# Attention beside a dense branch on one core: key tiles through one query half, then the other, seven score units beside twelve products, and a division on 128x32 sums

## The chip, the core and the metric

One of the cores of a Trainium2 chip runs the whole kernel. Its engines are TensorE (PE; PEld are its weight loads, which run beside the products), VectorE (DVE), ScalarE (ACT), GpSimd (POOL), and SyncE (SP), which issues most of the DMAs. Each engine works off its own queue in order, and semaphores let one wait for another. Products go to PSUM, eight banks of 128 x 512 floats. The metric is the device time of one execution in microseconds. All times below are from one profile and three runs of the kernel before; "a unit", "a phase" and "a pair" are explained with the kernel.

## The reference

Two branches on the same input x (2048 rows, 512 columns) are mixed by a gate. Branch A is attention with 32 query heads of 16 columns and one shared key and value head; branch B is a dense layer, a squared ReLU, and a second dense layer.

```python
def _A_ref(x, wq, wk, wv, wo):          # H = 32, Dh = 16
    q = (x @ wq).reshape(B, S, H, Dh).transpose(0, 2, 1, 3)
    k = x @ wk
    v = x @ wv
    scores = jnp.einsum("bhqd,bkd->bhqk", q, k) * (Dh ** -0.5)
    p = _softmax(scores, axis=-1)
    o = jnp.einsum("bhqk,bkd->bhqd", p, v)
    return o.transpose(0, 2, 1, 3).reshape(B, S, H * Dh) @ wo
def _B_ref(x, w1, b1, w2, b2):          # F = 1792
    h = jnp.einsum("bsd,df->bsf", x, w1) + b1
    r = jnp.where(h > 0, h, 0)
    return jnp.einsum("bsf,fd->bsd", r * r, w2) + b2
x = A_x
g = _sigmoid((x * gate_w).sum(-1, keepdims=True))
return g * _A_ref(x, ...) + (1 - g) * _B_ref(x, ...)
```

## The kernel before

**Attention.** The 2048 queries lie in four chunks of 512, the 32 heads in eight groups of four: 32 iterations (`it`, `NC * NG`), and in each 16 key tiles of 128 keys (`kt`). A **unit** `u` is one key tile with one half of the 512 queries (256 columns) for all four heads, so an iteration has 32 units and the kernel 1024 (`place`, L738). In every iteration but the last, a key tile's two halves follow each other; in the last, all key tiles run through the first half and then through the second.

A unit's scores are two products of 49 rows (`score`, L753), one in each half of the rows of TensorE's array (r = 0 and r = 1), which run beside each other; each half holds two heads. They go to a PSUM tile `s` of two banks (two of them take turns), and ScalarE writes their exponentials to SBUF (`exps`, L781). Some units are "raw": each half goes to the single bank `x`, VectorE copies it to SBUF (`score_copy`, L770), and ScalarE then exponentiates in place. The exponentials lie in five tiles `e` of two units each. The contexts (`context`, L797) multiply them with the values and a column of ones (`v_ext`), for the four heads beside each other in four groups of the array's columns, and add up in one bank `acc`: heads in rows 32h and on, values and sums of the exponentials in alternating rows. Before, two units of one key tile share products of 512 columns.

**The other products.** The queries' projection (15 pieces), the dense branch and the output projection are split into a rounded part and the rest (`split`, L191; names ending in r and l), so that a tile needs three products for each pair of tiles. A piece of this work with one PSUM bank `mm` (a span, `Span`) has 12 products, some have 9, the last ones fewer. A product of 128 rows is done in two halves of 64 rows: the first half of one span runs beside the second half of the span before, so a step of TensorE is always a **pair** of row halves, either of products or of scores.

**The order.** `manual_schedule` keeps each engine's instructions as they are written. The program is a sequence of **phases** (`phase`, L1138): the scores of some units and the products of a span, interleaved by a table (`PLANS`; M is a product, S0 a unit's scores, 02 and 12 the two halves of raw unit 2), and behind them the contexts of as many units, which were scored up to four units ahead (`AHEAD`). `block` (L1191) chooses how many units and products a phase takes: six or four units here, and no phase crosses the end of an iteration. A planner keeps rough clocks (`at_pe`, `at_act`, `at_dve`) and puts VectorE's other work (`spend`, L622: rests of weights, chores, divisions) between the copies of raw scores. Work for DMAs has due times (`LANDS`, `DIVIDES`, `WRITES`).

**The division.** When an iteration ends, `finish` (L836) copies acc to SBUF on ScalarE; two DMAs take the values to `oc` and the sums of exponentials to `lc`, one row of 512 sums for every row of values (the sums of a head stand 16 times). After two iterations `divide` (L821) works on six slices of at most 86 columns: bound the sums, compare with what was bounded (its count, `ok`, tells at the end whether the shift of the exponents sufficed), reciprocal, product with the values. A POOL DMA writes `oc` to DRAM (`oTs`), from where the output projection reads.

Of the kernel before, what the change touches and what calls it, by code (L numbers as in the profile page):

```python
# [10 lines left out]
F32 = mybir.dt.float32  # L11
# [12 lines left out]
NG = 8  # L24
# [10 lines left out]
PARTS = [slice(a, min(a + 86, CH)) for a in range(0, CH, 86)]  # L35
LANDS, DIVIDES, WRITES, SURE = 6.0, 10.0, 14.0, 0.7
# [20 lines left out]
LAST_OK = (NC * KT - 1) * len(PARTS)  # L57
# [106 lines left out]
def mix_kernel(ctx: ExitStack, tc: tile.TileContext, xT, wkv, wq, wo, w12, b1, b2, cst, out):  # L164
# [7 lines left out]
    qs = dram.tile([NC * NG, 2, KS, 2, CH], F32, name="qs")  # L172
    oTs = dram.tile([NC * NG, 64, CH], F32, name="oTs")
# [7 lines left out]
    ok = keep.tile([128, NC * KT * len(PARTS)], F32, name="ok")  # L181
# [46 lines left out]
    with fast, tc.tile_pool(name="at", bufs=1) as at, \  # L228
# [381 lines left out]
        def later(f, *args):  # L610
            chores.append((1.2, lambda: f(*args)))
# [85 lines left out]
        def x_again(c):  # L697

            r, l = [xp.tile(sh, F32R, name=f"x{n}again{c}", tag=f"x{n}{c - 2}") for n in "rl"]
            def load(a):  # L700
                nc.sync.dma_start(stage()[:, :2], xT[c, 2 * a:2 * a + 2].rearrange("k p s -> p k s"))
                return LANDS

            def part(k):
                split(r[:, k], l[:, k], stage()[:, k % 2])
                if k == KT - 1:
                    x[c] = r, l

            for k in range(KT):
                if k % 2 == 0:  # L710
                    chores.append((0.0, lambda k=k: load(k // 2)))
                later(part, k)
# [84 lines left out]
        def context(acc, us):  # L797

            nonlocal at_pe
            at_pe += 0.12  # L800
            while us:
                u, (it, kt, q) = us[0], place(us[0])
                n = 2 if u % 2 == 0 and len(us) > 1 and it < NC * NG - 1 else 1
                at_pe = max([at_pe] + [made[i] + 0.06 for i in us[:n]]) + CONTEXT * n
                us = us[n:]
                cols, mine = slice(q * HC, (q + n) * HC), slice(u % 2 * HC, (u % 2 + n) * HC)
                for h in range(4):
                    nc.tensor.matmul(acc[h * 32:(h + 1) * 32, cols], v_ext[:, kt],  # L808
                                     es[u // 2][:, h % 2 * 2 + h // 2, mine], start=(kt == 0), stop=(kt == NK - 1),
                                     skip_group_check=True, tile_position=(0, h * 32))  # L810
            if narrow:
# [9 lines left out]
        def divide(o, l, cols, okc):  # L821

            n = []

            def bound():
                n.append(at.tile([128, 86], F32, name="n")[:, :cols.stop - cols.start])
                nc.vector.tensor_scalar(n[0], l[:, cols], L_MIN, L_MAX, op0=OP.max, op1=OP.min)

            def compare():
                nc.vector.scalar_tensor_tensor(l[:, cols], n[0], 1.0, l[:, cols], op0=OP.mult, op1=OP.is_equal,  # L830
                                               accum_out=okc)

            return ((0.23, bound), (0.35, compare), (0.72, lambda: nc.vector.reciprocal(n[0], n[0])),  # L833
                    (0.28, lambda: nc.vector.tensor_tensor(o[:, cols], o[:, cols], n[0], OP.mult)))

        def finish(it, acc):  # L836

            c, gr = divmod(it, NG)
            t, u = divmod(gr, 2)
            if it == NC * NG - 2:  # L840
                a = at.tile([128, CH], F32, name="al", tag="accs")
                nc.vector.tensor_copy(a, acc)
                side.append(turn(a, 0, range(4), LAST_OK))
                return
            a = at.tile([128, CH], F32, name="accs")
            nc.scalar.activation(a, acc, AF.Copy)
            act(0.62, at_pe)
            if u == 0:
                ol[c, t] = [at.tile([128, CH], F32, name=n, bufs=2) for n in ("oc", "lc")]
            o, l = ol[c, t]  # L850
            unpack(nc.sync, o[u * 64:u * 64 + 64], l[u * 64:u * 64 + 64], a)
            if u == 1:
                for q, cols in enumerate(PARTS):
                    i = len(PARTS) * (4 * c + t) + q
                    divisions.extend((d, at_act + (LANDS if (c, t) == (NC - 1, 2) else DIVIDES), f) for d, f in divide(o, l, cols, ok[:, i:i + 1]))

                def done():
                    nc.gpsimd.dma_start(oTs[it - 1:it + 1].rearrange("u d n -> (u d) n"), o)
                    complete.add((c, t))

                divisions.append((0.0, 0.0, done))
# [27 lines left out]
        def half(acc, q):  # L889
# [3 lines left out]
            nc.vector.tensor_copy(a[:, :HC], acc[:, q * HC:q * HC + HC])  # L893
# [21 lines left out]
            if q:  # L915
                nc.vector.tensor_scalar(bad, pf, 128.0 * ((NC * KT - 1) * CH + 32) - 0.5, None, op0=OP.is_lt)
# [14 lines left out]
        def o_ready(c):  # L931

            if c == 0 and not wos:
                wos.extend(xp.tile(sh, F32R, name=n, tag=t) for n, t in (("wor", "xr2"), ("wol", "xl2")))

                def load(a):
                    nc.sync.dma_start(stage()[:, :2], wo[a * 256:a * 256 + 256].rearrange("(t p) n -> p t n", p=128))
                    return WRITES

                for t in range(KT):  # L940
                    if t % 2 == 0:
                        chores.append((0.0, lambda t=t: load(t // 2)))
                    later(split, wos[0][:, t], wos[1][:, t], stage()[:, t % 2])
            if c > 0:
                ask(c - 1)

        def ask(c, n=KT):
# [15 lines left out]
            def part(t):  # L963
                orr, orl = tiles
                split(orr[:, t], orl[:, t], stage()[:, t % 2])
                if t == n - 1:
                    osp[c] = orr, orl

            for t in range(n):
                if t % 2 == 0:  # L970
                    chores.append((0.0, lambda t=t: load(t // 2)))
                later(part, t)

        def ask_one(c, t):
# [10 lines left out]
            def part():  # L985
                split(osp[c][0][:, t], osp[c][1][:, t], stage()[:, 0])
                osp[c, t] = True

            chores.extend(((0.0, load), (1.2, part)))
# [23 lines left out]
        def work():  # L1013
# [61 lines left out]
            units_left[0] = 0  # L1075
# [5 lines left out]
        side, units = [], work()  # L1081
# [108 lines left out]

        def block(u):  # L1191
# [8 lines left out]
            if span.done[0] == 0 and left > 9:  # L1200
                halved[0] += max(0.0, (total - 20 - u - 6 * units_left[0]) / (1.6 * max(units_left[0], 1)))
            if rest == 8 or rest == 4 or left > 9 and halved[0] >= 1.0 and rest not in (6, 10) and not late:
                halved[0] -= 1.0
                return 4, (left + 1) // 2
            return min(rest, 6), left

        late, halved, units_left = [], [0.5], [NC * (NF + 16) + 15 + 16]

        acc, us = None, ()
# [9 lines left out]
        u = 0  # L1219
        while u < total:  # L1220
            it, k = divmod(u, 2 * NK)
            if k == 0 and it + 1 < NC * NG:
                q_load(it + 1)
# [8 lines left out]
            if k == 0:  # L1232
                acc = ap.tile([128, CH], F32, name="acc")
            context(acc, range(u, u + m))
            u += m
            if u % (2 * NK) == 0 and it < NC * NG - 1:
                finish(it, acc)
            if u == total - NK:
                side.append(half(acc, 0))
                next(side[-1])  # L1240
# [51 lines left out]
```

## Time and profile before

| what | value |
|---|---|
| median of 3 runs | 1217.73 us (1217.41 to 1217.99) |
| the profiled execution | 1217.18 us, span 1215.4 us |
| TensorE's granted clock | 0.999 of full speed |
| HBM traffic | 57.83 MB read, 20.97 MB written, 65 GB/s |
| contexts (L808) | 4224 product records, two for each product |
| scores to s (L757), to x | 1640, 408 |
| exponentials from PSUM, in place (L794) | 820, 204 |

The page's rows name a line, an engine, an operation, what it writes and reads (out<-in), a shape and a count; then busy time, the mean of one, and the engine's idle time before them with what ended it. In the chain in order of time, a row is a start, a length and what the program was waiting for then. TensorE's products overlap, so a start minus the start before tells what one costs, not its duration.

### The profile page before, as it was taken

What the parts mean: (1) busy time and instruction counts of PE and PEld (TensorE: products, weight loads), DVE (VectorE), ACT (ScalarE), POOL (GpSimd) and SP (SyncE); (2) the same over time, 40 slices, a digit from 0 to 9 for tenths busy, and PEclk for the clock granted to TensorE, in tenths of its full rate; (3) what the DMA queues carried; (4) which work ended last, traced back from release to release, by engine and by line L of the source; (5) the groups of instructions that cost most, each with busy time, mean ns of one, the idle gap of its engine ahead of it and who ended that gap; (6) DMA issues with size and microseconds to landing.
All of it is one profiled execution on the core that took longest, in us unless ns stands there. A gap on an engine that the chain in (4) does not pass through costs nothing.

```text
span 1215.4 us, 24123 instructions
## 1 busy us (share of the span) xinstructions
PE 1204.3 (99%) x9846; PEld 667.1 (55%) x9846; DVE 773.7 (64%) x1518; ACT 1035.5 (85%) x1145; POOL 65.3 (5%) x87
## 2 busy tenths in 40 slices
PE   9999999999999999999999999999999999999997
PEld 4555555555555555555555555555555555555554
DVE  6765778567774865737757673756747577574633
ACT  6788888898888889888988888888988888888875
POOL 1000120000002000000002001000010000000000
PEclk9999999999999999999999999999999999999999
DMA  6344432121222233101313212112121223211011
GB/s 230 80 115 107 108 92 66 58 66 49 72 73 93 75 75 100 57 20 58 109 49 127 68 51 92 49 40 57 58 88 49 75 66 80 63 43 48 23 53 38
DMA packets 45348, 88.71 MB, mean 73 GB/s; under 512 B 10643, under 2 KB 10899, under 8 KB 44721
## 3 DMA queue, kind: packets, MB, share of 16 engines
q1 hardware_dynamic: 37024, 68.27, 18.5%
q0 software_dynamic: 8064, 18.59, 5.0%
q8 instruction: 79, 1.29, 0.4%
q14 instruction: 37, 0.30, 0.1%
q10 hardware_dynamic: 144, 0.26, 0.1%
HBM read 57.83 MB, written 20.97 MB: 65 GB/s over the span
## 4 chain that ended last, share of the span: by engine, by line
PE 93%; ACT 3%; DVE 2%; DMA 1%; issue 1%; SPq 0%; ACTq 0%; DVEq 0%
PE acc L808 36%; PE mm L1111 33%; PE s L757 17%; PE x L757 6%; ACT e L794 2%; DMA qa<-qs 1%; PE mm L296 0%; PE acc L526 0%; PE mm L200 0%; ACT w1r L497 0%; DVE e L778 0%; DMA w1f<-in_w 0%; DVE qr L392 0%; DVE sq L396 0%; PE s L306 0%
## 5 line engine op out<-in xcount | busy, mean ns | idle before, releaser
L794 ACT ACTIVATE e<-s 128x1024 f32<-128x1024 f32 x820 | 780.0, 1025 | 155.6 <-PE s L757 154.5
L778 DVE COPY e<-x 128x512 f32<-128x512 f32 x408 | 281.6, 690 | 377.7 <-PE x L757 332.9
L808 PE MATMUL acc<-e,v_ext 128*32 128x512 f32 (+1 forms) x4224 | 483.0, 584 | 0.0
L757 PE MATMUL s<-qa,k_aug 49*128 49x512 f32 x1640 | 459.8, 412 | 0.2
L757 PEld LDWEIGHTS s<-qa,k_aug 49*128 49x128 f32 x1640 | 233.4, 185 | 77.5 <-ACT e L794 54.6
L808 PEld LDWEIGHTS acc<-e,v_ext 128*32 128x32 f32 x4224 | 115.7, 109 | 240.8 <-issue 236.9
L794 ACT ACTIVATE e<-e 128x1024 f32<-128x1024 f32 x204 | 216.8, 1063 | 0.8 <-DVE e L778 0.8
L1111 PE MATMUL mm<-w2r,hr 64*128 64x512 f32 x752 | 172.3, 402 | 0.0
L757 PE MATMUL x<-qa,k_aug 49*128 49x512 f32 x408 | 166.1, 407 | 1.3 <-DVE o L884 0.7
L1111 PEld LDWEIGHTS mm<-w2r,hr 64*128 64x128 f32 x752 | 110.5, 186 | 41.8 <-DVE hr L193 7.5
L757 PEld LDWEIGHTS x<-qa,k_aug 49*128 49x128 f32 x408 | 75.8, 186 | 50.8 <-issue 11.7
L1111 PE MATMUL mm<-w2l,hr 64*128 64x512 f32 x376 | 90.7, 392 | 0.0
L1111 PE MATMUL mm<-xlagain,w1r 64*128 64x512 f32 x224 | 71.2, 391 | 0.0
L1111 PE MATMUL mm<-xragain,w1r 64*128 64x512 f32 x224 | 70.8, 417 | 0.4
L1111 PE MATMUL mm<-xl,w1r 64*128 64x512 f32 x224 | 69.3, 391 | 0.0
L1111 PE MATMUL mm<-xr,w1r 64*128 64x512 f32 x224 | 68.8, 416 | 0.3
L833 DVE RECIPROCAL n<-n 128x86 f32<-128x86 f32 x90 | 61.4, 683 | 1.6
L1111 PE MATMUL mm<-more 64*128 64x512 f32 x216 | 60.5, 394 | 0.0
L1111 PEld LDWEIGHTS mm<-w2l,hr 64*128 64x128 f32 x376 | 57.2, 186 | 3.7
L1111 PEld LDWEIGHTS mm<-xragain,w1r 64*128 64x128 f32 x224 | 37.8, 185 | 28.2 <-DVE big L664 5.0
L1111 PEld LDWEIGHTS mm<-xr,w1r 64*128 64x128 f32 x224 | 37.0, 185 | 26.9 <-DVE big L664 6.7
L1111 PE MATMUL mm<-xragain,w1l 64*128 64x512 f32 x224 | 50.5, 392 | 0.0
(169 smaller groups left out, 1254.0 us busy)
## 6 DMA issues: line engine op xcount, KB each, us to landing
stage<-in_w SPq DMA_DIRECT2D x56, 256.0 KB
qa<-qs SPq DMA_DIRECT2D x186, 64.0 KB
w1f<-in_w SPq DMA_DIRECT2D x28, 256.0 KB
w2f<-in_w SPq DMA_DIRECT2D x28, 256.0 KB
qs<-qr SPq DMA_DIRECT2D x16, 256.0 KB
ress<-res POOLq DMA_DIRECT2D x4, 1024.0 KB, 4.4
qs<-ql POOLq DMA_DIRECT2D x15, 256.0 KB, 7.8
oc<-accs SPq DMA_DIRECT2D x30, 128.0 KB
```

The lines of the kernel that those rows point to most:

```text
L757: nc.tensor.matmul(dst.rearrange("p (a n) -> p a n", a=2), k_aug[rows, kt * 128:(kt + 1) * 128], qa[it][rows, :, q * HC:q * HC + HC], star ...
L778: nc.vector.tensor_copy(e_half(u)[:, 2 * r:2 * r + 2], x.rearrange("p (a n) -> p a n", a=2))
L794: nc.scalar.activation(e_half(u), src, AF.Exp, scale=SCALE)
L808: nc.tensor.matmul(acc[h * 32:(h + 1) * 32, cols], v_ext[:, kt], es[u // 2][:, h % 2 * 2 + h // 2, mine], start=(kt == 0), stop=(kt == NK ...
L833: return ((0.23, bound), (0.35, compare), (0.72, lambda: nc.vector.reciprocal(n[0], n[0])), (0.28, lambda: nc.vector.tensor_tensor(o[:, co ...
L1111: nc.tensor.matmul((self.before if r else self).bank, a[p], b[p], start=not r and i == 0, stop=r == 1 and i == len(self.terms[1]) - 1, ski ...
```

## The change

It does four things. All iterations but the first run their 16 key tiles through one query half and then through the other (`place`); only the first still takes the halves in turn, with products of 512 columns. A phase may end anywhere in an iteration, and the copy of acc goes half by half, each when its last key tile is done (`context`, `finish`). A new table row takes seven units beside twelve products, two of them raw; `block` takes it unless a share of the remaining work (`halved`) asks for six or four, and `exact` fills the first iteration and the last 16 units by the cheapest mix. And the division takes only one of the 16 equal rows of sums: 512 sums of eight heads go to a tile `lq` of 128 x 32; bound, compare and reciprocal run on that; one POOL DMA writes the result to DRAM (`ls`), eight more read each head's row back to 16 partitions of `lc`, and one product of 128 x 512 multiplies it with the values. The splits of chores (`later`) become two chores each.

```diff
-PARTS = [slice(a, min(a + 86, CH)) for a in range(0, CH, 86)]
-LANDS, DIVIDES, WRITES, SURE = 6.0, 10.0, 14.0, 0.7
+LW = 4 * CH // 64
+LANDS, DIVIDES, WRITES, SPREADS, SURE = 6.0, 10.0, 14.0, 8.0, 0.7
...
+EXACT = {12: ((7, 12), (6, 12), (4, 6)), 9: ((6, 9), (4, 5))}
 PLANS = {
+    (7, 12, WHOLE): ("14 S0 M M S1 M M 04 M M S2 M M 13 M M M S5 M S6 03", (0, 1, 2, 4, 5, 3, 6)),
...
-        def later(f, *args):
-            chores.append((1.2, lambda: f(*args)))
+        def later(r, l, src, then=None):
...
+            chores.extend(((0.46, cast), (0.71, rest)))
...
-            return (it, k // 2, k % 2) if it < NC * NG - 1 else (it, k % NK, k // NK)
+            return (it, k % NK, k // NK) if it else (it, k // 2, k % 2)
...
-        def context(acc, us):
+        def context(us):
...
+            for u in us:
+                it, kt, q = place(u)
...
+                n = 1
+                if it == 0:
+                    if q == 0:
+                        continue
+                    q, n, u = 0, 2, u - 1
+                accs[q] = both[0][:, q * HC:q * HC + HC * n]
                 for h in range(4):
...
+                if kt == NK - 1:
+                    finish(it, q)
...
-        def divide(o, l, cols, okc):
...
+        def divide(o, l, i, ready):
+
+            n = at.tile([128, LW], F32, name="n")
+            wide = at.tile([128, CH], F32, name="lc", bufs=2)
+
+            def over():
+                nc.vector.reciprocal(n, n)
+                nc.gpsimd.dma_start(ls[i].rearrange("a (b n) -> (a b) n", b=16), n)
+                for k in range(8):
+                    nc.gpsimd.dma_start(wide[16 * k:16 * k + 16], bass.AP(tensor=ls.tensor, offset=ls[i, k].offset,
+                                                                          ap=[[0, 16], [1, CH]]))
+
+            return ((0.1, ready, lambda: nc.vector.tensor_scalar(n, l, L_MIN, L_MAX, op0=OP.max, op1=OP.min)),
+                    (0.2, ready, lambda: nc.vector.scalar_tensor_tensor(l, n, 1.0, l, op0=OP.mult, op1=OP.is_equal,
+                                                                        accum_out=ok[:, i:i + 1])),
+                    (0.3, ready, over),
+                    (0.72, ready + SPREADS, lambda: nc.vector.tensor_tensor(o, o, wide, OP.mult)))
...
+            nc.scalar.activation(a[:, q * HC:q * HC + HC], accs[q], AF.Copy)
+            act(0.41, at_pe)
+            if q == 0:
+                return
...
+            nc.sync.dma_start(l[u * 64:u * 64 + 64], a[1:128:32].rearrange("h (b n) -> h b n", n=LW))
...
-            rest = NK - u % NK if u >= total - 2 * NK else 2 * NK - u % (2 * NK)
-            left = span.left()
+            rest, left = total - u, span.left()
...
+            if rest <= 16 or u < 32:
+                return exact(min(rest, 32 - u) if u < 32 else rest, left, late or u < 18)
+            if left <= 9:
+                return 6, left
...
+                return 4, 6
+            return 7, left
...
-        while span.unit or units_left[0]:
-            fetch()
-            phase(span.slots, 0, 0)
-        for _ in half(acc, 1):
+        while span.left() or span.unit or not ended:
+            if not span.left():
+                fetch()
+            phase(span.left(), 0, 0)
+        for _ in half(accs[1], 1):
```

On TensorE, in the middle of the dense branch, the second half of a phase of the kernel before (s and x are scores, mm products of a span, acc contexts; two halves of a pair read as one row with x2):

```order
L1111 MATMUL mm<-xragain_3711,w1r 128x512 x2
L1111 MATMUL mm<-xlagain_3712,w1r 128x512 x2
L1111 MATMUL mm<-xragain_3711,w1r 128x512 x2
L757 MATMUL s<-qa,k_aug 128x512 x2
L1111 MATMUL mm<-xlagain_3712,w1r 128x512 x2
L1111 MATMUL mm<-xragain_3711,w1l 128x512 x4
L757 MATMUL s<-qa,k_aug 128x512 x2
L757 MATMUL x<-qa,k_aug 128x512
L1111 MATMUL mm<-xragain_3711,w1l 128x512 x4
L757 MATMUL s<-qa,k_aug 128x512 x2
L808 MATMUL acc<-e,v_ext 32x512 x12
```

And the second half of a phase of seven units at the same place of the changed kernel:

```order
L1141 MATMUL mm<-xragain_4099,w1r 128x512 x2
L1141 MATMUL mm<-xlagain_4100,w1r 128x512 x2
L1141 MATMUL mm<-xragain_4099,w1l 128x512
L765 MATMUL x<-qa,k_aug 128x512
L1141 MATMUL mm<-xragain_4099,w1l 128x512 x4
L765 MATMUL s<-qa,k_aug 128x512
L1141 MATMUL mm<-xragain_4099,w1l 128x512 x2
L765 MATMUL s<-qa,k_aug 128x512 x2
L1141 MATMUL mm<-xragain_4099,w1l 128x512
L765 MATMUL x<-qa,k_aug 128x512
L765 MATMUL s<-qa,k_aug 128x512
L824 MATMUL acc<-e,v_ext 32x256 x28
```

The row halves are shifted by one step against each other, two x products stand in this half and not one, and the contexts are 28 products of 256 columns (seven units) where 12 of 512 (six units) stood. Counted over the program, TensorE has 210 groups of contexts before and 157 now: 100 phases of seven units beside twelve products, 7 of seven beside twelve and nine, 31 of six beside nine, 7 of six beside twelve, 9 of four, and three small ones at the end.

On VectorE, a stretch of one division before (L827 bounds, L830 compares, L833 and L834 divide; L778 copies raw scores, L663 to L193 are the eviction of a hidden tile, L483 and L492 split weights):

```order
L827 TENSOR_SCALAR n<-lc 128x86
L830 SCALAR_TENSOR_TENSOR lc,ok<-n,lc 128x86
L778 COPY e<-x 128x2x256
L663 TENSOR_SCALAR big<-mm,b1t 128x512
L664 TENSOR_TENSOR big<-big 128x512
L192 CAST hr<-big 128x512
L193 TENSOR_TENSOR hr<-big,hr 128x512
L492 TENSOR_TENSOR w1l<-w1f,w1r 128x512
L778 COPY e<-x 128x2x256
L833 RECIPROCAL n<-n 128x86
L778 COPY e<-x 128x2x256
```

And one whole division now (L786 copies raw scores, L675 to L196 are the eviction, L495 splits weights):

```order
L857 TENSOR_SCALAR n<-lq 128x32
L858 SCALAR_TENSOR_TENSOR lq,ok<-n,lq 128x32
L851 RECIPROCAL n<-n 128x32
L786 COPY e<-x 128x2x256 x2
L675 TENSOR_SCALAR big<-mm,b1t 128x512
L676 TENSOR_TENSOR big<-big 128x512
L195 CAST hr<-big 128x512
L196 TENSOR_TENSOR hr<-big,hr 128x512
L786 COPY e<-x 128x2x256
L495 TENSOR_TENSOR w1l<-stage,w1r 128x512
L786 COPY e<-x 128x2x256
L861 TENSOR_TENSOR oc<-oc,lc 128x512
```

Two copies, an eviction, a copy, a weight's rest and another copy now stand between the reciprocal and the product; the product reads lc, which DMAs write. Behind it in the queue are the next two copies of raw scores.

On POOL, the queue around one division (L217 and L221 are the output projection's, L895 the result's way to DRAM):

```order
L217 DMA big<-ress 128x512
L221 DMA out<-big 128x512
L852 DMA ls<-n 128x32
L854 DMA lc<-ls 16x512 x8
L221 DMA out<-big 128x512
L895 DMA oTs<-oc 128x512
```

The write and the eight reads are new; before, only the L895 row stood there for a division.

More of the change, by code (lines that the diff above doesn't have):

```diff
@@ L819, in mix_kernel @@
         complete = set()
-        def divide(o, l, cols, okc):
[L823 to L834, printed above, removed]
@@ L838, in finish @@
+        sums = []
+        def finish(it, q):
             c, gr = divmod(it, NG)
             t, u = divmod(gr, 2)
+            if it == NC * NG - 1:
+                if q == 0:
+                    side.append(half(accs[0], 0))
+                    next(side[-1])
+                return
+            if q == 0:
+                sums.append(at.tile([128, CH], F32, name="accs"))
+            a = sums[-1]
             if it == NC * NG - 2:
-                a = at.tile([128, CH], F32, name="al", tag="accs")
@@ L842, in finish @@
-                nc.vector.tensor_copy(a, acc)
-                side.append(turn(a, 0, range(4), LAST_OK))
+                nc.vector.tensor_copy(a[:, q * HC:q * HC + HC], accs[q])
+                if q:
+                    side.append(turn(a, 0, range(4), LAST_OK))
                 return
-            a = at.tile([128, CH], F32, name="accs")
-            nc.scalar.activation(a, acc, AF.Copy)
-            act(0.62, at_pe)
+            nc.scalar.activation(a[:, q * HC:q * HC + HC], accs[q], AF.Copy)
@@ L983, in load @@
                 return LANDS
[L985 to L989, printed above, removed]
+            chores.append((0.0, load))
+            later(lambda: osp[c][0][:, t], lambda: osp[c][1][:, t], lambda: stage()[:, 0],
+                  lambda: osp.update({(c, t): True}))
         used, over = [False] * NC, set()
@@ L1074, in work @@
                 yield terms(j, KT - 1, *last[0]), done, None
-            units_left[0] = 0
+            ended.append(True)
         def terms(j, t, r, l):
@@ L1079, in terms @@
             return pairs(r[:, cols], l[:, cols], wos[0][:, t], wos[1][:, t])
-        side, units = [], work()
+        side, units, ended = [], work(), []
         total = NC * NG * 2 * NK
@@ L1189, in phase, with exact, price @@
                         w_round(half, nc.vector.tensor_copy)
+        def exact(rest, slots, later):
+            def price(rest, size, later):
+                if rest == 0:
+                    return 0.0, None
+                options = []
+                for m, n in EXACT[size]:
+                    parts = [n] if n == size or rest == 4 else [n, size - n]
+                    if m * len(parts) <= rest and not (later and m == 7):
+                        t = sum(TURN + CONTEXT * m + PAIR * m for k in parts)
+                        options.append((t + price(rest - m * len(parts), 12, False)[0], (m, n)))
+                return min(options, default=(1e9, (min(rest, 6), size)))
+            return price(rest, slots, later)[1]
         def block(u):
-            rest = NK - u % NK if u >= total - 2 * NK else 2 * NK - u % (2 * NK)
-            left = span.left()
+            rest, left = total - u, span.left()
             if span.slots < 7 or left < 7:
@@ L1231, in mix_kernel @@
             phase(slots, min(u + m + AHEAD, total) - scored, m)
-            if k == 0:
-                acc = ap.tile([128, CH], F32, name="acc")
-            context(acc, range(u, u + m))
-            u += m
[L1236 to L1240, printed above, removed]
+            it = (u + m - 1) // (2 * NK)
+            if it not in begun_q and it + 1 < NC * NG:
+                begun_q.add(it)
+                q_load(it + 1)
+            context(range(u, u + m))
+            u += m
         while side:
```

88 lines of the change are left out of this document (47 added, 41 removed).

## The prediction

> **What bounds the kernel now.** I read the page's busy shares first, then its chain that ended last, then that chain in order of time in a steady stretch, and the groups of instructions for the engines that could become late.
>
> ```profile
> span 1215.4 us, 24123 instructions
> PE 1204.3 (99%) x9846; PEld 667.1 (55%) x9846; DVE 773.7 (64%) x1518; ACT 1035.5 (85%) x1145; POOL 65.3 (5%) x87
> ...
> PE 93%; ACT 3%; DVE 2%; DMA 1%; issue 1%; SPq 0%; ACTq 0%; DVEq 0%
> PE acc L808 36%; PE mm L1111 33%; PE s L757 17%; PE x L757 6%; ACT e L794 2%; DMA qa<-qs 1%; PE mm L296 0%; PE acc L526 0%; PE mm L200 0%; ACT w1r L497 0%; DVE e L778 0%; DMA w1f<-in_w 0%; DVE qr L392 0%; DVE sq L396 0%; PE s L306 0%
> ```
>
> A busy share of 99% can hide slack in a pipelined engine, so it is the second pair of rows that counts: 93% of the chain is TensorE, in its own order. The chain in order of time shows what one phase costs. A phase begins where a group of context products (acc) ends.
>
> ```profile
> 483.37 2.71 PE acc L808 x24
> 486.08 0.43 PE mm L1111 x2
> 486.51 0.23 PE x L757
> 486.74 0.23 PE s L757 x2
> ...
> 487.45 0.92 PE mm L1111 x8
> ...
> 490.51 2.71 PE acc L808 x24
> ...
> 495.80 1.85 PE acc L808 x16
> ...
> 500.18 1.85 PE acc L808 x16
> ```
>
> Eight products in 0.92 us are four pairs of row halves, so a pair is 0.23 us. The groups of 24 and of 16 records (six and four units; each product has two records) differ by 0.86 us, so a unit's context is 0.43. From 483.37 to 490.51 a phase of six units and twelve products took 7.14 us: 6 x 0.43, and 18 pairs (12 products, 6 scores) x 0.232, leave **0.38 us for turning** from scores to contexts and back (the first pair behind a group shows 0.43 in place of 0.23). From 495.80 to 500.18 a phase of four units and ten pairs took 4.38 us, which leaves 0.34. The turn hardly depends on the size of the phase.
>
> **The change part by part.** *Fewer phases.* Scores, products and context columns are the same in number. In the program's order, the groups of contexts on TensorE are 210 before and 157 now; 53 turns fewer x 0.38 = **-20.1 us**. A seven-unit phase beside twelve products should take 7 x 0.43 + 19 x 0.232 + 0.38 = 7.8 us.
>
> *Contexts of 256 columns.* Every context outside the first iteration now goes in two halves, with twice as many products and weight loads. The last iteration of the kernel before already works so:
>
> ```profile
> 1178.92 2.73 PE acc L808 x48
> ...
> 1202.23 2.73 PE acc L808 x48
> 1204.96 0.54 PE s L927 x2
> ...
> 1205.51 0.45 PE x L875 x2
> ...
> 1205.98 0.18 DVE nl L880
> ...
> 1206.18 0.18 DVE nl L881 x2
> ...
> 1206.38 0.21 DVE nl L883
> ```
>
> Six units take 2.73 us there against 2.71, so the 30 iterations that change cost 30 x 32 / 6 x 0.02 = **+3.2 us**. The weight loads stay hidden.
>
> *The end.* Nine half products of the last two units of the work now stand behind the last context, and their two evictions ahead of the copy of the last sums on VectorE. Before, 0.55 us pass from the end of the last context (1202.23 + 2.73) to the first transposition (1205.51). Now a turn, three pairs and their latency (1.1), an eviction and a look at the bank (0.75 + 0.15, see the L1048 row below), three products (1.0), an eviction (0.75) and the copy (0.5) take 4.2. Of the 3.7 us difference, 1.4 are products that left the phases: **+2.3 us**.
>
> *The division.* Six slices of 86 columns become one of 32, and the reciprocals spread by DMA.
>
> ```profile
> L778 DVE COPY e<-x 128x512 f32<-128x512 f32 x408 | 281.6, 690 | 377.7 <-PE x L757 332.9
> L833 DVE RECIPROCAL n<-n 128x86 f32<-128x86 f32 x90 | 61.4, 683 | 1.6
> ...
> 488.05 0.20 DVE L827 TENSOR_SCALAR n<-lc 128x86 f32<-128x86 f32 x1
> 488.28 0.25 DVE L830 SCALAR_TENSOR_TENSOR lc<-n,lc 128x86 f32<-128x86 f32 x1
> 488.45 0.08 DVE L830 DVE_READ_ACCUMULATOR lc<-n,lc 128x1 f32 x1
> ...
> 501.88 0.43 DVE L192 CAST hr<-big 128x512 fp32r<-128x512 f32 x1
> ...
> 1199.67 0.75 DVE L1048 SCALAR_TENSOR_TENSOR ot<-mm,g,most 128x512 f32<-128x512 f32 x1 [2.21 <-PE mm L1111]
> ```
>
> VectorE saves 75 of its 90 reciprocals (about 51 us) and as many of the small steps around them, and gets 116 more copies of raw scores (524 for 408 in the order, x 0.69 = 80 us). That is near a draw on an engine that TensorE seldom waits for, so I count it at **0**; what hides it is VectorE's idle third (64% busy), and were that gone, each late copy of raw scores would hold up TensorE for its whole delay. What counts is the wait that comes with it. On VectorE the product with the spread reciprocals (oc<-oc,lc) waits for nine POOL DMAs issued after the reciprocal: one write of the 32 columns to DRAM, then, once that has landed, eight reads of 16 partitions. The price of this chain, from rows of the same queue:
>
> ```profile
> 726.39 0.24 DVE L834 TENSOR_TENSOR oc<-oc,n 128x82 f32<-128x82 f32 x1
> ...
> 727.04 0.56 POOL L858 DMA_DIRECT2D oTs<-oc  x1 [71.29 <-DVE oc L834]
> ...
> 12.19 1.96 POOL L383 DMA_DIRECT2D qa<-qr  x4 [10.21 <-ACT qr L376]
> ...
> 469.63 0.55 POOL L218 DMA_DIRECT2D out<-big  x1 [30.55 <-DVE big L217]
> 472.32 0.54 POOL L214 DMA_DIRECT2D big<-ress  x1 [2.14 <-DMA out<-big]
> ...
> qa<-nrm POOLq DMA_DIRECT2D x2, 2.0 KB, 2.3
> big<-ress POOLq DMA_DIRECT2D x12, 256.0 KB, 4.0
> ```
>
> From VectorE's end to POOL's start are 0.41 us (726.63 to 727.04). From a write's issue to the issue of a read that waits for it are 2.69 (469.63 to 472.32). Four DMAs to 16 partitions x 512 took 1.96, so each is 0.49, and the eighth read starts 3.43 after the first. It lands 2.3 (2 KB) to 4.0 (256 KB, from DRAM) later; 32 KB is nearer to the small one, I take 2.6. Sum 0.41 + 2.69 + 3.43 + 2.6 = **9.1 us**, with 8.8 and (0.54 an issue, 4.0) 10.9 as ends.
>
> Against that stands what VectorE has to do in between. At ten of the fifteen divisions the order puts the reciprocal behind a phase's second raw copy and the product behind the second raw copy of the next seven-unit phase: one period of 7.8 us, less about 0.8 for the bound, the compare and the reciprocal on 32 columns (0.20 + 0.33 + 0.68 on 86 columns by the rows above; 0.18 + 0.18 + 0.21 on 8 columns by the L880 to L883 rows of the kernel's end), so **7.0 us**. VectorE then stands for 9.1 - 7.0 = 2.1 us, and behind it in its queue is the third raw copy, whose bank TensorE needs six pairs after it was written. That bank has little slack:
>
> ```profile
> 620.30 0.50 PE L757 MATMUL x<-qa,k_aug 49*128 49x512 f32 x1
> 620.83 0.69 DVE L778 COPY e<-x 128x512 f32<-128x512 f32 x1 [1.01 <-PE x L757]
> ...
> 621.58 0.50 PE L757 MATMUL x<-qa,k_aug 49*128 49x512 f32 x1
> ```
>
> From one x product to the next 1.28 us are needed (620.30 to 621.58), six pairs are 1.39: with the gap before the copy some 0.3 us can be absorbed. So TensorE loses 1.8 us at each of ten places, 18 us. Three places leave 5.5 to 6.5 us but more slack behind, together some 4; two leave 8 or more and cost nothing. **+22 us**, with 15 + 3 and 36 + 8 as ends.
>
> On prices, the Trainium skill's page "DMA: Bandwidth & Descriptors", section "Anatomy of one DMA — SWDGE (gpsimd) path", gives 2.0 us + bytes / 436e3 for a DMA of this queue. By it both landings are about 2.05 and the chain is about 8.3 us, the loss 12 and not 22; the 4.0 row above is slower than the page's 2.6 for 256 KB.
>
> *Raw scores.* Two of seven units and not one of six are exponentiated in place.
>
> ```profile
> L794 ACT ACTIVATE e<-s 128x1024 f32<-128x1024 f32 x820 | 780.0, 1025 | 155.6 <-PE s L757 154.5
> L794 ACT ACTIVATE e<-e 128x1024 f32<-128x1024 f32 x204 | 216.8, 1063 | 0.8 <-DVE e L778 0.8
> L497 ACT ACTIVATE w1r<-w1f x22: 614/630/660, 69.8 to 1006.4; 128x512 fp32r<-128x512 f32 x22
> ```
>
> Back to back one from PSUM costs 780.0 / 820 = 0.95 us, one in place 1.06: 5 x 0.95 + 2 x 1.06 = 6.9 us of ScalarE in 7.8. The order has 100 roundings of weights on ScalarE (0.63 each) where it had 64, about two in three phases, and two half copies of the sums an iteration. That makes 7.5 of 7.8. A phase whose first unit is odd also waits for a buffer of e, the sixth tile of five, till the first context ends; there is about half a microsecond before TensorE feels it. I take **+2 us**, from 0 to 20.
>
> **Sum.** 1215.4 - 20.1 + 3.2 + 2.3 + 22 + 2 = 1224.8 us of span. The profiled execution took 1217.18 us, 1.8 over its span, and the median of the runs is 0.5 over that: **1227 us**.
>
> **The rivals.** *A, the forecast:* the spread reciprocals come late and cost more than the turns bring; chance 0.50, 1220 to 1234. *B, the chain is covered:* were it to end within 7.3 us, the 22 would be gone and the time 1205. For it speaks that each DMA alone lands in 2.3; against it, that the reads wait for the write, and the eight issues are one after another. It decides at 7.3 us; chance 0.20, 1202 to 1215. *C, a partial cover:* a chain of 8.3 to 8.5 us loses about 12 to 14, so 1217 to 1219, no change; chance 0.17. *D, a longer chain:* the reads queue behind VectorE's casts in SBUF, one or two of 0.43 us stand between in most places; that adds up to 0.9 at ten places, 1236; chance 0.08. The same skill's page "SBUF — State Buffer", section "SBUF: two separate sides", states that a VectorE copy from SBUF to SBUF locks GpSimd out of writing descriptors; the trace's POOL issues in the rows above, 0.49 to 0.56, show little of it. *E, ScalarE becomes the bound:* with 7.5 of 7.8 us taken, 0.2 us more in each of the 107 seven-unit phases cost 21 us, 1246 with the forecast's wait and 1226 without; the four-unit phases before (3 x 0.95 + 1.06 in 4.38, 89%) speak against it; chance 0.05.
>
> **How the numbers follow.** A, D and E are slower: 0.63. C is within 0.2% (1215.3 to 1220.2, about what a measurement can tell): 0.17. B is faster: 0.20. The likeliest gives 1227. The range takes in C and D, half of B, and all but the uppermost of the chain's bounds (36 + 8 would give 1249): 1206 to 1245. A's own is 1220 to 1234.
>
> **What would show it.** Right: 157 context groups, phases of 7.8 us, 2.73 us for six halved units; product oc<-oc,lc on VectorE waiting about 2 us for the DMA lc<-ls in most of fifteen places, with an x product on TensorE idle behind it. Wrong: no such idle time, or the last lc landing within 7.3 us of the reciprocal; seven-unit phases over 8 us without a division, with e or s waiting for ScalarE, would be E.

## The result, and the profile after

The changed kernel takes 1386.51 us (median of 4 runs, 1383.44 to 1395.2), the kernel before on the same chip 1217.57 (4 runs): a ratio of 1.140, 95% interval 1.135 to 1.145. The forecast said 1227, slower by 0.8%; it is slower by 14%. The profiled run took 1385.57 us, its span 1383.8. First the rows of its page that answer to those shown of before: engines' busy times, the granted clock in 40 slices, and the chain by engine ("issue" there is time in which an engine waited for nothing that the profile shows).

```profile
span 1383.8 us, 31763 instructions
PE 1246.4 (90%) x13686; PEld 801.9 (58%) x13686; DVE 742.4 (54%) x1221; ACT 1060.9 (77%) x1211; POOL 132.4 (10%) x222
...
PEclk9999899999999999999998999999999999999999
...
PE 46%; issue 34%; ACT 11%; POOL 4%; DMA 3%; DVE 2%; DVEq 0%; POOLq 0%; ACTq 0%
```

TensorE stands idle for 137 us of its span (11 before), and no engine fills that time: ScalarE's share fell from 85% to 77%, VectorE's from 64% to 54%, and POOL, which got the new DMAs, is at 10% (5% before). So nothing is overloaded; something is waited for. The view of waits of the changed kernel (who waited for whom: us in total, times, longest) names it:

```profile
PEld acc L824 <- ACT accs L882: 144.3, 52, 7.0
PE acc L824 <- ACT accs L882: 119.3, 52, 6.6
...
PEld s L765 <- ACT e L802: 48.6, 123, 0.8
...
DVE oc L861 <- DMA lc<-ls: 13.1, 9, 4.1
```

The wait of the forecast (VectorE for the spread reciprocals) is there, with 13 us. The large one stands in no term of it: at 52 places a context product waits for ScalarE's copy of a half of the sums (`accs`), 2.3 us on average. The chain in order of time shows one of them, between two phases of seven units:

```profile
339.39 3.16 PE acc L824 x56
...
347.18 0.61 PE acc L824 x8
347.79 0.02 issue
347.81 0.02 ACTq L802
347.83 0.04 issue
347.87 0.13 ACT e L802
348.00 0.79 issue
348.79 1.96 ACT e L802 x2
350.76 0.52 ACT w1r L500
351.27 0.28 ACT accs L882
351.56 0.04 issue
351.60 4.07 PE acc L824 x48
355.67 0.43 PE s L765
```

The first phase needs 7.79 us from group to group (339.39 to 347.18), as forecast. In the second group one unit (8 records) ends a half, and six units (48 records) begin the other half. Between them lie 3.8 us in which TensorE does nothing. ScalarE's own rows in that time:

```profile
347.87 1.02 ACT L802 ACTIVATE e<-s 128x1024 f32<-128x1024 f32 x1 [0.78 <-PE acc L824]
348.79 1.05 ACT L802 ACTIVATE e<-e 128x1024 f32<-128x1024 f32 x1
349.74 1.01 ACT L802 ACTIVATE e<-s 128x1024 f32<-128x1024 f32 x1
350.64 0.63 ACT L500 ACTIVATE w1r<-stage 128x512 fp32r<-128x512 f32 x1
351.16 0.38 ACT L882 ACTIVATE accs<-acc 128x256 f32<-128x256 f32 x1
```

The copy itself takes 0.38 us. It waits for its turn in ScalarE's queue, behind three exponentials and a rounding that the rest of this group doesn't need; the first of them had itself waited for a buffer of `e` that the contexts had to free. TensorE in turn has its next context in the same PSUM bank and waits for the copy; the scores and products of the next phase, which could run, stand behind that context in its own queue.

And the idle time costs twice. The six units behind it took 4.07 us, not 2.73. Windows around them (the window and its length; busy us of PE, PEld, VectorE, ScalarE and POOL with the number of instructions; then the granted clock, DMA share, GB/s):

```profile
342.50:347.20 4.70, 4.70 (x46) 3.73 (x46) 2.83 (x5) 4.03 (x5) 0.00 (x0) 1.00 0.19 59
347.80:351.60 3.80, 0.00 (x0) 0.00 (x1) 2.58 (x5) 3.67 (x5) 0.00 (x0) 0.90 0.00 0
351.60:355.70 4.10, 4.10 (x50) 1.93 (x50) 0.00 (x0) 0.00 (x0) 0.00 (x0) 0.68 0.00 0
355.70:360.00 4.30, 4.30 (x35) 3.59 (x35) 2.67 (x4) 3.56 (x4) 0.00 (x0) 1.00 0.26 75
```

The granted clock falls to 0.68 behind the idle time. At full clock a record takes 0.057 us (2.73 / 48); worked out from the starts behind all these waits, the rest of the groups took 45 us more than that. 119 us of waiting and 45 us of slow products are 164 us.

The kernel before has the same copy, on the same engine, and nobody feels it. Its rows (TensorE's contexts, and ScalarE's copy between them) at the end of an iteration:

```profile
508.91 1.92 PE L808 MATMUL acc<-e,v_ext 128*32 128x512 f32 x16
...
510.90 0.60 ACT L846 ACTIVATE accs<-acc 128x512 f32<-128x512 f32 x1
...
515.21 2.78 PE L808 MATMUL acc<-e,v_ext 128*32 128x512 f32 x24
```

The copy ends at 511.50, and the next context comes at 515.21: the next phase's scores and products lie between, 3.7 us of cover. That cover is what "phases end anywhere" took away.

### The profile page after: what moved, and what is told of

Read it like the earlier page. It is cut to its first block, busy times and chain, and to the rows that moved or that the text cites. A ratio compares the mean times of both kernels' runs of the same rounds, so it can differ in the third digit from the quotient of the medians.

```text
span 1383.8 us, 31763 instructions
## 1 busy us (share of the span) xinstructions
PE 1246.4 (90%) x13686; PEld 801.9 (58%) x13686; DVE 742.4 (54%) x1221; ACT 1060.9 (77%) x1211; POOL 132.4 (10%) x222
## 4 chain that ended last, share of the span: by engine, by line
PE 46%; issue 34%; ACT 11%; POOL 4%; DMA 3%; DVE 2%; DVEq 0%; POOLq 0%; ACTq 0%
PE acc L824 19%; PE mm L1141 14%; PE s L765 9%; ACT e L802 9%; PE x L765 2%; POOL lc L854 2%; DMA ls<-n 1%; DMA lc<-ls 1%; POOL res L697 1%; ACT accs L882 1%; DVE e L786 1%; ACT w2r L500 1%; POOL qs L358 1%; DVE oc L861 0%; ACT w1r L500 0%
## 5 line engine op out<-in xcount | busy, mean ns | idle before, releaser
L802 ACT ACTIVATE e<-s 128x1024 f32<-128x1024 f32 x762 | 749.2, 1027 | 288.1 <-PE s L765 234.6
L786 DVE COPY e<-x 128x512 f32<-128x512 f32 x524 | 362.4, 692 | 573.5 <-PE x L765 461.9
L824 PE MATMUL acc<-e,v_ext 128*32 128x256 f32 (+1 forms) x8064 | 528.3, 410 | 120.9 <-ACT accs L882 119.3
L824 PEld LDWEIGHTS acc<-e,v_ext 128*32 128x32 f32 x8064 | 252.9, 115 | 357.7 <-ACT accs L882 144.3
L765 PE MATMUL s<-qa,k_aug 49*128 49x512 f32 x1524 | 444.8, 418 | 0.1
L802 ACT ACTIVATE e<-e 128x1024 f32<-128x1024 f32 x262 | 277.1, 1058 | 5.8 <-DVE e L786 5.7
L765 PE MATMUL x<-qa,k_aug 49*128 49x512 f32 x524 | 221.7, 423 | 6.3 <-DVE e L786 4.0
L765 PEld LDWEIGHTS x<-qa,k_aug 49*128 49x128 f32 x524 | 97.9, 187 | 35.2 <-DVE e L786 10.6
L854 POOL DMA_DIRECT2D lc<-ls x120 | 58.3, 494 | 30.9 <-DMA ls<-n 30.7
L1141 PE MATMUL mm<-xr,w1l 64*128 64x512 f32 x224 | 50.5, 392 | 0.0
```

The costliest lines, as they stand in the source:

```text
L765: nc.tensor.matmul(dst.rearrange("p (a n) -> p a n", a=2), k_aug[rows, kt * 128:(kt + 1) * 128], qa[it][rows, :, q * HC:q * HC + HC], star ...
L786: nc.vector.tensor_copy(e_half(u)[:, 2 * r:2 * r + 2], x.rearrange("p (a n) -> p a n", a=2))
L802: nc.scalar.activation(e_half(u), src, AF.Exp, scale=SCALE)
L824: nc.tensor.matmul(accs[q][h * 32:(h + 1) * 32], v_ext[:, kt], es[u // 2][:, h % 2 * 2 + h // 2, u % 2 * HC:u % 2 * HC + HC * n], start=(k ...
L854: nc.gpsimd.dma_start(wide[16 * k:16 * k + 16], bass.AP(tensor=ls.tensor, offset=ls[i, k].offset, ap=[[0, 16], [1, CH]]))
L1141: nc.tensor.matmul((self.before if r else self).bank, a[p], b[p], start=not r and i == 0, stop=r == 1 and i == len(self.terms[1]) - 1, ski ...
```

## The experiments

Three theories. **Q**: contexts wait in the middle of a group for a half copy that stands in ScalarE's queue. **O**: seven units with two raw ones overload ScalarE (rival E of the prediction). **D**: VectorE's wait for the spread reciprocals (the forecast's term) is all there is, and larger than thought. Each run is compared with the kernel before on the same chip.

**The copies read a constant.**

```diff
-            nc.scalar.activation(a[:, q * HC:q * HC + HC], accs[q], AF.Copy)
+            nc.scalar.activation(a[:, q * HC:q * HC + HC], cs[:, C_ONE:C_ONE + 1].to_broadcast([128, HC]), AF.Copy)
```

> The copies of the half sums read a column of ones in place of acc; nothing else changes, and the contexts' results are left out of the output. ScalarE has as much to do as before in the same order. Theory Q (TensorE waits in the middle of a context group for the half copy, which stands behind exponentials in ScalarE's queue): no context waits for accs any more, the stalls of about 184 us (1383.8 of span, less 1215.4 - 20.1 + 3.2 + 2.3 = 1200.8) fall to 0 to 25, time 1203 to 1230. Theory O (ScalarE is overloaded by seven-unit phases with two raw units): nothing is taken off ScalarE, so 1350 or more. Theory D (VectorE's wait for the spread reciprocals): that wait stays, 1350 or more.

Measured: 1229.12 us (1.011, 1.007 to 1.015), 157.4 us under the changed kernel. ScalarE is as busy as there, but the page has TensorE at 98%:

```profile
PE 1193.8 (98%) x13686; PEld 786.5 (64%) x13686; DVE 742.4 (61%) x1221; ACT 1058.3 (87%) x1211; POOL 131.7 (11%) x222
```

With 1058 us of ScalarE's work in a span of 1222.8, O falls, and so does D, for VectorE's wait for `lc` is still there (26.6 us in 14 places). Q holds: the edit takes away the dependency between contexts and copy, and no work. What is left is 2.1 us over the forecast's 1227.

**And the division's product reads a constant too.**

```diff
-                    (0.72, ready + SPREADS, lambda: nc.vector.tensor_tensor(o, o, wide, OP.mult)))
+                    (0.72, ready + SPREADS, lambda: nc.vector.tensor_tensor(o, o, cs[:, C_ONE:C_ONE + 1].to_broadcast([128, CH]), OP.mult)))
```

> As c_ones, and the product of each division reads a column of ones in place of lc, so that VectorE waits for no spreading DMA (the DMAs are still issued). The sums, the contexts and the division's result are left out of the output. The difference to c_ones is the price of the wait that was forecast at 22 us (bounds 18 and 44); if the chain is covered or absorbed, the difference is under 3 us.

Measured: 1206.05 us (0.990, 0.988 to 0.992), and TensorE is at 99%:

```profile
PE 1187.1 (99%) x13686; PEld 786.1 (65%) x13686; DVE 742.5 (62%) x1221; ACT 1057.5 (88%) x1211; POOL 132.4 (11%) x222
```

The wait for the spread reciprocals costs 23.1 us by the medians; the two intervals together leave 18 to 33, and the two profiled executions differ by 18.7 us of span (1222.8 and 1204.1). The forecast's 22 holds as a sum, but it is made up differently. In the run before (the copies read a constant, the wait is there) VectorE's rows of its first division, with POOL's queue:

```profile
120.60 0.70 POOL L358 DMA_DIRECT2D qs<-ql  x1 [8.17 <-DVE n L851]
121.28 0.59 POOL L852 DMA_DIRECT2D ls<-n  x1
129.29 3.88 POOL L854 DMA_DIRECT2D lc<-ls  x8 [7.42 <-DMA ls<-n]
...
135.45 0.69 DVE L861 TENSOR_TENSOR oc<-oc,lc 128x512 f32<-128x512 f32 x1 [7.40 <-DMA lc<-ls]
...
136.80 0.79 PE L765 MATMUL x<-qa,k_aug 49*128 49x512 f32 x1 [4.54 <-DVE e L786]
```

and of a later one:

```profile
492.81 0.35 DVE L851 RECIPROCAL n<-n 128x32 f32<-128x32 f32 x1
...
493.57 0.55 POOL L852 DMA_DIRECT2D ls<-n  x1 [4.58 <-DVE n L851]
495.65 3.84 POOL L854 DMA_DIRECT2D lc<-ls  x8 [1.53 <-DMA ls<-n]
...
501.12 0.69 DVE L861 TENSOR_TENSOR oc<-oc,lc 128x512 f32<-128x512 f32 x1 [0.87 <-DMA lc<-ls]
...
502.46 0.49 PE L765 MATMUL x<-qa,k_aug 49*128 49x512 f32 x1 [0.38 <-DVE e L786]
```

In the later one the write is read back after 2.08 us (493.57 to 495.65), the eighth read is issued 3.4 later and lands within 2, 7.8 us from the reciprocal's end. In the first one the write of 16 KB was issued 0.7 us behind one of 256 KB (`qs<-ql`) and was read back only after 8.0 us: VectorE waits 7.4 us there. In the run with the constant the same write stands 1.1 us behind the large one and is read back after 7.5; in the changed kernel it stands 4.0 us behind it, and it takes 5.1. That fits a wait behind the large DMA, but no run took that DMA away. Compared phase by phase with the run without the wait, the phase with this division takes 8.2 us more (16.09 against 7.94), and ten others take 0.5 to 2.2 more each, 10.9 together.

**The copies on VectorE.**

```diff
-            nc.scalar.activation(a[:, q * HC:q * HC + HC], accs[q], AF.Copy)
-            act(0.41, at_pe)
+            nc.vector.tensor_copy(a[:, q * HC:q * HC + HC], accs[q])
+            dve(0.42, at_pe)
```

> The half copies run on VectorE in place of ScalarE, where before them stand the phase's last raw copy and an eviction. The wait of the contexts for the copy stays. Theory Q: the wait shrinks to a copy of 0.42 us and what is left of VectorE's queue, 0.6 to 1.8 us at 58 places, 35 to 104 us over 1203: 1238 to 1307. Theory O: ScalarE is relieved of 60 copies of 0.38 us, 23 us at most: 1360 or more.

Measured: 1308.65 us (1.077, 1.072 to 1.081), 78 under the changed kernel and 1.7 over the range's upper end: the slow products were not in that estimate. The same contexts wait, now for the other engine:

```profile
PE acc L824 <- DVE accs L882: 74.3, 52, 7.9
```

So the dependency stays with whichever engine copies, and its price is that engine's queue. Behind these waits the slow products take 16 us.

**The copies earlier in ScalarE's queue.** Exponentials that the rest of the group doesn't need before the half's end, and that would run past it, are emitted behind the copy (cut to its core; `phase` fills `hold` with the half's last unit and its planned end):

```diff
             while todo:
                 u = todo[0]
+                if hold and u > hold[0][0] and at_act + EXP > hold[0][1]:
+                    return
...
                 if kt == NK - 1:
                     finish(it, q)
+                    if hold:
+                        hold.clear()
+                        exps(kept)
```

> In phases with a half's end inside their context group, the exponentials that the group doesn't need before that end and that would, by the planner's clock, run past it are emitted behind the half copy: 1.6 of them on average for each of the 60 copies. All work is done. Theory Q in its form 'the queue ahead of the copy': the copy runs some 1.6 us earlier, so 52 x 1.6 = 83 us or somewhat more come back, 1270 to 1315. If only the dependency as such counts (the copy's own length and the semaphores), the time stays within 1% of the changed kernel's 1386.

Measured: 1274.72 us (1.048, 1.045 to 1.051), 112 under the changed kernel with the same engine and dependency; 1.6 exponentials a copy moved. The work is the same in sum; the planner gave ten roundings of weights to ScalarE that VectorE had before. Its view of waits, and one copy in its time:

```profile
PE acc L827 <- ACT accs L889: 38.9, 52, 1.7
```

```profile
328.98 0.64 PE L827 MATMUL acc<-e,v_ext 128*32 128x256 f32 x8
...
329.89 0.37 ACT L889 ACTIVATE accs<-acc 128x256 f32<-128x256 f32 x1
...
330.32 2.80 PE L827 MATMUL acc<-e,v_ext 128*32 128x256 f32 x48 [0.70 <-ACT accs L889]
```

No wait is over 1.7 us, and the products behind lose 5 us in all, 2.1 of them at one place (138.56) where TensorE had just stood idle 5.65 us for a raw copy. At the place shown TensorE takes 2.80 us for the 48 records. The 45.6 us that this run lies over the one without the dependency (1274.72 - 1229.12) are close to those 39 + 5. The shortest wait, 0.50 us, little more than the copy itself, is met at some 30 of the 52 places. At the place shown the wait is 0.70 us: 0.27 until the copy starts, 0.37 for the copy, 0.06 until the next product.

**Phases that end with the iteration.** `place` gives a key tile's two halves in turn again (but in the last iteration), and `block` picks the cheapest mix that ends where the iteration does: mostly 7, 7, 7, 7, 4 units and then 4, 7, 7, 7, 7. Two units of one key tile share context products of 512 columns again, as in the kernel before. That makes 169 groups of contexts, and both half copies stand at the end of one. So this run takes back the 256 columns (3.2 us in the forecast) together with the place of the copies.

```diff
-            return (it, k % NK, k // NK) if it else (it, k // 2, k % 2)
+            return (it, k // 2, k % 2) if it < NC * NG - 1 else (it, k % NK, k // NK)
...
+                n = 2 if u % 2 == 0 and len(us) > 1 and it < NC * NG - 1 else 1
...
-                n = 1
...
+            rest = NK - u % NK if rest <= 2 * NK else 2 * NK - u % (2 * NK)
...
-            if rest <= 16 or u < 32:
-                return exact(min(rest, 32 - u) if u < 32 else rest, left, late or u < 18)
...
+            return exact(rest, left, late or u < 18)
```

> Key tiles' halves in turn again (but for the last iteration), and phases end at each iteration's end, with seven units beside twelve products where that fits (169 context groups, 92 of them of seven units beside a span of twelve); the copies of both halves stand at a group's end. Division and ScalarE's work as in the changed kernel. Theory Q: no wait in the middle of a group, 41 turns of 0.38 us fewer than before = -15.6, +2.3 for the end, and 0 to 20 for the division's wait: 1204 to 1224. Theory O: 92 of the 107 seven-unit phases remain, so at least 1340.

Measured: 1231.40 us (1.012, 1.009 to 1.014), 155 under the changed kernel with 92 of 107 seven-unit phases kept, so O falls a second time; but 7 over the range's upper end. No context waits for a copy in the middle of the work any more. What is left shows in its view of waits:

```profile
DVE oc L857 <- DMA lc<-ls: 28.9, 11, 6.3
```

The expectation had put the division's wait at 0 to 20. So the next edit gives the DMAs more time:

```diff
-LANDS, DIVIDES, WRITES, SPREADS, SURE = 6.0, 10.0, 14.0, 8.0, 0.7
+LANDS, DIVIDES, WRITES, SPREADS, SURE = 6.0, 10.0, 14.0, 20.0, 0.7
```

> c_iter with the product of the division due 20 us behind the reciprocal in the planner's clock, not 8: 6 to 11 raw copies stand between the two where 4 or 5 stood. Theory D (what c_iter has left is VectorE's wait for the spread reciprocals): the wait of 28.9 us in 11 places goes but for a remainder at the first division, whose write took 6 us: 1231.4 - 23 = 1205 to 1213. If the rest of c_iter is something else (an uneven mix of phases, weights late), it stays at 1225 or more.

> As c_iter_s20 with 24 us: 8 to 14 copies between. Theory D: also the first division's wait is gone, so 0 to 4 us less than c_iter_s20, unless the last division's product now comes too late for the output projection.

Measured: with 20 us 1212.27 us (0.9952, 0.9936 to 0.9969), with 24 us 1212.38 (0.9954, 0.9935 to 0.9973). The first is 19.1 under the run with 8 us, as its expectation has it, and no VectorE row waits for `lc` any more; the longer time adds nothing. The page of the run with 20 us:

```profile
span 1209.5 us, 24987 instructions
PE 1192.0 (99%) x10285; PEld 675.2 (56%) x10286; DVE 741.4 (61%) x1222; ACT 1050.5 (87%) x1202; POOL 133.4 (11%) x222
```

This kernel computes all of the output and is faster than both, by 0.5% against the kernel before (its interval excludes 1, though the gain is small). 41 fewer turns of 0.38 would have given 15.6 us; some 5 us go to its end, where 9.9 us lie between the last context and the last product (4.7 before): 15 half products stand behind the last context there (none in the kernel before, 9 in the changed kernel). Where the other 5 went stays open.

## Why the prediction was wrong

**Fewer phases: right.** Undisturbed seven-unit phases take 7.79 us (forecast 7.8), and with both waits taken away the span is 1204.1, against 1215.4 - 20.1 + 3.2 + 2.3 = 1200.8 (1202.8 with the 2 for raw scores).

**Contexts of 256 columns, the end: right.** Six halved units take 2.73 us. From the last context's end to the span's end it is 14.3 us in that run and 10.4 before, 3.9 more (forecast 3.7).

**The division: right in the sum, by luck; not in its make-up.** Forecast 22, measured 23.1. In the run with the wait the chain is 7.6 to 8.4 us at eleven of the fifteen divisions, not 9.1; with the constant in place of `lc` the product starts 7.0 to 7.5 us behind the reciprocal's end at eleven of them (forecast 7.0). So all places but one cost 11 to 15 us together, near rival C's 12. The rest, some 8 us, is that one place, the first division, which the forecast priced as it did the others although a DMA of 256 KB had been issued in the same queue just before. On the landing time the Trainium skill's page "DMA: Bandwidth & Descriptors", section "Anatomy of one DMA — SWDGE (gpsimd) path", was nearer than the row chosen: by it 2.05 us, and the trace has 1.9 to 2.1 for most reads; the write of the first division, which landed 7.7 us after its issue, is far from it. (The prediction's chain of 8.3 us by that page is not the sum of its terms: 0.41 + 2.05 + 3.43 + 2.05 = 7.9.)

**Raw scores: within the range.** Between the run without both waits and the terms above lie 3.3 us; the forecast had 2, from 0 to 20. VectorE's work, called near a draw, fell by 31 us (773.7 to 742.4). Rival E (whose 1246 should be 1248 by its own figures, 1227 + 21) is refuted: with ScalarE's work unchanged the time falls to 1229.

**What failed: the half copies had no term of their own.** The prediction's list goes through fewer phases, 256 columns, the end, the division and raw scores; "phases may end anywhere" has no entry. The copies appear once, under raw scores, as "two half copies of the sums an iteration", counted as ScalarE's work inside "7.5 of 7.8". Who waits for a copy, and what stands ahead of it in its queue, was not asked, and among the signs only e or s waiting for ScalarE was named, not acc. The term it lacked is 157.4 us, 3.0 at each of 52 places: 2.3 of waiting and 0.9 of slow products, less what the slower kernel saves elsewhere (VectorE's wait for `lc`, 26.6 us in 14 places without the copies' wait, is 13.1 in 9 with it). The rows to see it by were in the profile of before: the copy at 510.90 ends 0.7 us behind the contexts, and is hidden by the 3.7 us until the next context; a group that goes on in the same bank has no such cover, and the phase's exponentials and roundings stand ahead of the copy.

Why two halves of a bank are one resource is what the Trainium skill's page "PSUM — Partial Sum Buffer" states in its section "PSUM bank collisions raise a hardware error": accesses of two engines must be kept apart by bank and quadrant, not by address. The program waits accordingly: each of the 52 context groups that go on behind a half's end waits for that half's copy, though it writes the other 256 columns. What would happen without the wait was not tried, and a second bank for the other half was not either: scores, raw scores, products and contexts fill all eight. The sign, slower, would have come out without this too, and by the wait that was forecast: 1229.12 us is 1.1% over the kernel before, and 1206.05 without that wait is 1.0% under it. But of the 11.7 us that lie above it, 8.2 are the first division's, which the forecast didn't see.

## What to carry to other kernels

When an edit moves the end of a group, ask of each copy out of PSUM what ran between it and the next write to that bank, and what will run there now: a copy of 0.4 us costs its engine's queue, here 2.3 us on average and 0.9 of slow products behind it, and holds up all that stands behind the waiting product. Larger phases paid off only where the copy stayed at a phase's end, and where the DMAs that a product waits for got two phases and not one. Price a small DMA in a queue shared with large ones at the busiest time at which it is issued.

## What the hardware showed that was not expected

The clock of TensorE fell behind shorter idle times than expected. In the changed kernel, behind waits of up to 1.87 us the rest of a group took no more than 0.11 us extra; behind 2.05 us and more it mostly took 0.4 to 2.5 extra, though not always (2.61 us at 290.6 cost 0.02). With the copies on VectorE, seven of the eight waits of 2.2 to 2.7 us cost nothing (0.09 at most). So the length of a wait doesn't decide alone. Two windows of the changed kernel, an idle time of 2.05 us and the products behind it:

```profile
894.40:896.50 2.10, 0.05 (x4) 0.00 (x0) 0.43 (x1) 2.05 (x3) 0.00 (x0) 1.00 0.01 2
896.50:900.50 4.00, 3.99 (x42) 1.82 (x42) 0.00 (x0) 0.00 (x0) 0.00 (x0) 0.57 0.02 4
```

The granted clock is 0.57 there. The Trainium skill's page "TensorE: Matmul & The Clock Gate", section "What's actually happening", puts the fall behind an idle window of about 3.4 us; here 2.05 us were enough at that place, and the measurement decides. The page adds that the window runs freely, so that the point of a change depends on where in it the first product lands.

The traces show such windows, and they explain the exceptions. In the record of the granted clock of each of the nine profiled executions, the changes lie on a grid of 3.413 us (to 0.003 us), and the low stretches have a clock of 0.5. What counts is TensorE's idle time within one window of that grid. In the changed kernel and in the two runs with the copies on VectorE or earlier in ScalarE's queue, up to the last few microseconds, every window at full clock with 2.05 us or more of idle time is followed by one at 0.5, and none with 1.80 or less is; between them both occur. The wait of 2.05 us shown above lies in one window (893.54 to 896.95), and the clock is 0.50 from 896.95 to 900.37. The wait of 2.61 us at 290.6 is cut by an edge at 289.38 into 1.43 and 1.18, and the clock stays at 1.00; the seven waits that cost nothing with the copies on VectorE are cut in the same way, into parts of 2.00 us at most. So in these three runs an idle time cost the clock when it took more than about half of one window, and not otherwise.
